# Lightning attention and four-expert MoE on one core: q and k of eight chunks rearranged in DRAM and turned on VectorE, with several smaller edits

## The chip, the cores and the metric

The kernel runs on one core of a Trainium2 chip, in FP32 throughout. A core has a matrix engine (TensorE, PE in the profile; its weight loads are the row PEld), three engines for elementwise work (VectorE or DVE, ScalarE or ACT, GpSimd or POOL), and SyncE (SP), whose queue issues nearly all DMA transfers of this kernel; 16 DMA engines carry them out. TensorE writes into PSUM, eight banks of 128 partitions x 512 FP32 values; DVE and ACT empty them. The metric is the time of one execution on the device in microseconds (us), as a median over runs.

## The reference

Two blocks in a row. The first is a decayed linear attention in blocks of 64 positions, for 4 batches, 8 heads, 768 positions and 64 features:

```
intra = einsum(qb, kb) * Dmask ; intra = einsum(intra, vb)
inter = einsum(qb * lam_pow, kv_state)
out[block] = intra + inter
kv_state = lam**64 * kv_state + einsum(kb * rev_pow, vb)
```

The second is a mixture of four experts with dense gates over the 3072 resulting tokens (512 wide, hidden width 1024):

```
p = domain_probs / (domain_probs.sum(-1) + 1e-9)
for e in range(4):
    out += p[:, e:e+1] * (relu(x @ w1[e]) @ w2[e])
```

## The kernel before

**Attention.** The kernel uses blocks of 128 positions (*chunks*), 6 to a batch, 24 in all. A chunk takes three steps on TensorE. `turn` (line 456) transposes its q and k, each [128 positions, 8 heads x 64], with four 128x128 transposes each into two PSUM banks; ACT copies them out as `qT` and `kT`, DVE makes the decayed `qs` (not for a batch's first chunk), and POOL decays k in place. `scores` (line 479) multiplies `kT` by `qT`, and DVE masks the result into `st`. `values` (line 497) multiplies `st` and the state by v, and the ACT copies bring the result into `xT`, the MoE's input of the present group. A *group* is 8 chunks, so there are three.

**MoE.** A *unit* is one group with one expert, twelve in all, numbered 0 to 11 by `at`. Both of its products (x by w1, and hidden by w2) are two-level Strassen-Winograd schemes with seven products M1 to M7 and sums of blocks as operands. The first product of unit n+1 is interleaved with the second product of unit n. For most units the seven operand sets of x and w1 are made ahead by POOL, stored in DRAM (`x_ops`, `w1_ops`), and read back one set at a time into two buffers (`xs_in`, `ws_in`; `feed`, line 658). Unit 0's first products are made directly from `xT` and from raw w1 blocks (`direct_product`, line 1063), and unit 1's from operands that are made for it in SBUF (`own`, line 1058, with the x sums of `own_x`, line 1004, on DVE). The last group (units 8 to 11) has a deeper scheme for the second product (`nested_product`).

**Order.** Everything is emitted by hand, and each engine runs its instructions in that order. A unit is seven *rounds* of eight *slots*. A slot emits a part of the products; then `rest` takes one item from a list of background work (DVE sums, masks, attention's DVE steps; `soon` puts items at its head), and `pump` takes POOL *chores* and DMA stores that are due. An attention step is placed in slot 5 of each round, and in slot 2 of rounds 1, 3 and 5 (line 1282). Group 1's attention runs in units 0 to 2, and group 2's in units 3 to 5. The SP queue is in order too: a transfer that waits for its buffer holds up those behind it.

**Opening.** The first ten iterations of the loop at line 1124 do group 0's attention with pieces of unit 0's direct products between. Iteration i has `turn` of chunk i, `scores` of chunk i-1 and `values` of chunk i-2, in this order, with `scores` ahead of `turn` in iteration 3 alone. Inputs are loaded in the order q and k of chunks 0 and 1, v0, q and k of 2, v1, q and k of 3, w1 block A11, v2, v3, then chunk 4, A12, chunk 5, A21, chunk 6, A22, chunk 7. In iteration 6 DVE makes the x operands of unit 1's M1 (line 1145). The rest of the direct products follows (lines 1181 to 1191, `SEQ0`).

**Later sums.** `finished` (line 679) queues the sums that follow products M6 and M7. In the last group one of the two operands is first copied into PSUM by ACT (`bring`, line 684), and DVE adds from there.

Of the kernel before, what the change touches and what calls it, by code (L numbers as in the profile page):

```python
# [22 lines left out]
def kernel(  # L23
# [320 lines left out]
    def sum_w1(e, name, a, b, op):  # L344
# [7 lines left out]
        w1_now[e][name] = to  # L352

    lam_bc = consts.tile([P, H], FP32, name="lam_bc")
    nc.scalar.dma_start(out=lam_bc[:], in_=lam.partition_broadcast(P))
    for n, names in ((0, "qk"), (1, "qk"), (0, "v"), (2, "qk"), (1, "v"), (3, "qk")):
        load(n, names)
    raw_w1(0, "A11")
    load(2, "v")
    load(3, "v")  # L360

# [88 lines left out]
    def soon(n, *work):  # L450

        background[0:0] = work
        if n < CPG:
            rest(len(work))

    def turn(n, tags):
        qn, kn = nat.pop((n, "q")), nat[n, "k"]
        qp = bank(tags[0], "qp")
        kp = bank(tags[1], "kp")
        for x, y in ((qp, qn), (kp, kn)):  # L460
            for ac in range(NHP):
                nc.tensor.transpose(  # L462
                    out=x[:, ac * C:(ac + 1) * C], in_=y[:, 2 * ac:2 * ac + 2].rearrange("p r d -> p (r d)"),
                    identity=ident[:],
                )
        qT, kT, qs = small("qT"), small("kT"), None
        nc.scalar.copy(out=qT[:], in_=qp[:])
        nc.scalar.copy(out=kT[:], in_=kp[:])
        if n % NCH:
            qs = small("qs")  # L470
            soon(n, lambda: tt(nc.vector, qs[:], qT[:], q_decay[:].rearrange("p h c -> p (h c)"), ALU.mult))
        turned[n] = qT, kT, qs
        if n % NCH < NCH - 1:

            kd = kn.rearrange("p (ac r) d -> p ac r d", r=2)
            by = k_decay.rearrange("p r ac -> p ac r").unsqueeze(3)
            tt(nc.gpsimd, kd, kd, by.to_broadcast([P, NHP, 2, D]), ALU.mult)

    def scores(n, tags):
        qT, kT, _ = turned[n]  # L480

# [58 lines left out]
    def attention(g):  # L540
# [3 lines left out]
        for n in range(g * CPG, (g + 1) * CPG):  # L544
            steps.append(lambda n=n: turn(n, ("s0", "s1")))
            steps.append(lambda n=n: scores(n, ("s0", "s1")))

            def end(n=n):
                if n == g * CPG:
                    for m in MS:  # L550
                        until(("x", g - 1, m))
                values(n, ("s0", "s1"))
                if n + AHEAD < B * NCH:
                    load(n + AHEAD)
                if n == g * CPG + CPG // 2 - 1:
# [123 lines left out]
    def finished(g, e, m, blocks, new):  # L679

        def later(to, a, b, order, relu=False):
            there = dict(a)

            def bring(at):

                there[at] = bank("s" + "01"[order.index(at) % 2], "up")
                nc.scalar.copy(out=there[at][:], in_=a[at][:])

            def step(at):
                x = there[at]  # L690
                if g == LAST and at != order[-1]:
                    bring(order[order.index(at) + 1])
                o = to[at] if at in to else small("m" + at)
                tt(nc.vector, o[:], x[:], b[at][:], ALU.add)
                if relu:
# [6 lines left out]
            blocks["left"] = 4  # L702
            if g == LAST:
                background.append(lambda: bring(order[0]))
            background.extend(lambda at=at: step(at) for at in order)
# [189 lines left out]
    def to_join(m):  # L895
# [5 lines left out]
        if m == "M3":  # L901
            steps(
                [(bring, "M1", 0, "q01")], [(bring, "M1", 1, "q02"), (add, "M6", "M1", 0)], [(add, "M6", "M1", 1)],
            )
# [99 lines left out]
    def own_x(m):  # L1004
# [14 lines left out]
        else:  # L1019
            if m == "M1":  # L1020
                s = [opool.tile([P, 2, 256], FP32, name="acc") for _ in range(2)]
                parts = ((1, 3), s[0][:]), ((3, 5), s[1][:])
                s = [x[:, i] for x in s for i in range(2)]
            else:
                s = stage.tile([P, 4, 256], FP32, name="ops", tag="st")
                parts = (((1, 5), s[:]),)
                s = [s[:, i] for i in range(4)]
            for n, x, y, op in T_OPS:
                b[n] = s[SLOT[n]]
                tt(nc.vector, b[n], b[x], b[y], op)  # L1030
            pieces = (
                ((0, 1), blk[:, 0:1, 0:256]), *parts, ((5, 7), blk[:, 1].rearrange("p (a f) -> p a f", a=2)),
            )
# [18 lines left out]

    own_ops, own_blocks = {}, {}

# [3 lines left out]
    def own(m):  # L1058
        if m not in own_ops:
            own_weights(m)  # L1060
        fed[0, 1, m] = own_blocks.pop(m, None) or own_x(m), own_ops[m]

    def direct_product(e, m, blocks, tags):

        settle(m, blocks)
        old = {"M1": None, "M5": None, "M6": "M1", "M2": "M1", "M7": "U2", "M3": "U4", "M4": "U3"}[m]
        new = {}

        def quarter(at):
            a, b = w1_now[e][A_OF[m]], x_now[B_OF[m]]  # L1070
            i, j = int(at[0]) - 1, int(at[1]) - 1
# [52 lines left out]
    for i in range(CPG + 2):  # L1124
# [29 lines left out]
        while more:  # L1154
            more.pop(0)()
# [17 lines left out]
    def sum_own(name, a, b, op=ALU.subtract):  # L1173
# [5 lines left out]
        raw["A12"],  # L1179
    ))  # L1180
    for m in SEQ0[2:]:
        if m == SEQ0[-1]:
# [34 lines left out]
    for at, (g, e) in enumerate(units):  # L1217
# [8 lines left out]
        if ahead and ahead[1] == 0:  # L1226
            assert not steps
            steps = attention(ahead[0] + 1) if ahead[0] + 1 < NG else []
        blocks, banks = {}, {}
        for i in range(7):  # L1230
# [30 lines left out]
            for x, part in enumerate(order):  # L1261
# [55 lines left out]
```

## Time and profile before

| What | Value |
|---|---|
| Median of 7 runs | 1196.13 us (1195.42 to 1198.0) |
| The profiled execution | 1197.44 us |
| Its span, first to last instruction | 1195.7 us |
| Busy share of the span: PE, DVE, ACT, POOL | 99%, 66%, 23%, 53% |
| Granted TensorE clock | 1.000 |
| Moved by DMA | 317.94 MB, 266 GB/s |
| Busy share of the 16 DMA engines, main queue (q1) | 77.7% |
| Transposes of q and k (L462), as recorded | 192 of 128x128 |

The share of busy time is over the whole span; which engine decides in a stage is read from the time slices and from the waits. A matrix instruction of the program that multiplies FP32 appears as two matmul records in the trace, and a transpose as one. Matmul records overlap, so the pitch of two starts says more than a record's length. The DMA share by slice lies between 0.4 and 0.99 for most of the run, highest between some 180 and 420 us.

### The profile page before, as it was taken

The numbers are of one execution on the slowest core, as the hardware profiler recorded it, in microseconds if no ns is written. First come the engines' busy times: TensorE is split into PE (matmuls) and PEld (weight loads), VectorE is DVE, ScalarE is ACT, GpSimd is POOL, SyncE is SP. The second block draws the span as 40 slices with busy tenths as digits, with TensorE's granted clock in tenths as the row PEclk, the third lists the DMA queues.
The fourth block names the chain that finished last, engine by engine and source line by source line (L and its number), as shares of the span: only waits on it lengthen the run. The fifth ranks groups of instructions, "written<-read, shape, count | busy, mean of one in ns | idle before, by whom it ended". The sixth has DMA issues, their size and how long they took to land.

```text
span 1195.7 us, 17929 instructions
## 1 busy us (share of the span) xinstructions
PE 1185.4 (99%) x6623; PEld 1030.9 (86%) x6623; DVE 789.6 (66%) x1318; ACT 278.9 (23%) x510; POOL 636.6 (53%) x600
## 2 busy tenths in 40 slices
PE   9999999999999999999999999999999999999998
PEld 8788888888888888888888888888888888888887
DVE  5698786477467746746764874774665676777784
ACT  3322122112212211211211120121243342341332
POOL 1885248349366810034524754416584593783884
PEclk9999999999999999999999999999999999999999
DMA  9794679999999985689977999898986657566542
GB/s 220 222 337 144 224 253 325 354 316 328 366 329 316 328 272 189 218 285 288 282 268 233 320 301 318 277 298 313 321 277 242 260 196 266 214 237 243 211 169 79
DMA packets 228135, 317.94 MB, mean 266 GB/s; under 512 B 91696, under 2 KB 169424, under 8 KB 228048
## 3 DMA queue, kind: packets, MB, share of 16 engines
q1 hardware_dynamic: 218496, 314.11, 77.7%
q10 hardware_dynamic: 9552, 2.69, 1.0%
q8 instruction: 52, 0.85, 0.3%
q14 instruction: 35, 0.29, 0.1%
HBM read 231.40 MB, written 85.34 MB: 265 GB/s over the span
## 4 chain that ended last, share of the span: by engine, by line
PE 92%; DVE 4%; SPq 1%; issue 1%; DMA 1%; POOL 0%; ACT 0%; ACTq 0%; DVEq 0%; POOLq 0%
PE pg L751 39%; PE q L805 32%; PE pq L977 13%; PE sp L485 2%; PE op L513 2%; DVE m L95 1%; DVE hS L95 1%; SPq L123 1%; PE op L508 1%; DVE xt L95 1%; PE op L521 1%; PE pM L1076 1%; PE qp L462 1%; PE kp L462 1%; PE pM L947 1%
## 5 line engine op out<-in xcount | busy, mean ns | idle before, releaser
L751 PE MATMUL pg<-xs_in,ws_in 128*128 128x256 f32 x1960 | 470.0, 380 | 0.5 <-DVE m L95 0.5
L751 PEld LDWEIGHTS pg<-xs_in,ws_in 128*128 128x128 f32 x1960 | 371.0, 190 | 52.3 <-DVE m L95 1.5
L95 DVE TENSOR_TENSOR m<-pg,m 128x512 f32<-128x512 f32 x451 | 308.5, 688 | 113.2 <-PE pg L751 103.9
L805 PE MATMUL q<-w2t,hS 128*128 128x256 f32 x1024 | 243.3, 380 | 0.0
L805 PEld LDWEIGHTS q<-w2t,hS 128*128 128x128 f32 x1024 | 192.9, 190 | 26.8 <-issue 0.3
L821 DVE SCALAR_TENSOR_TENSOR acc<-q,gate,acc 128x256 f32<-128x256 f32 x192 | 92.5, 482 | 178.3 <-PE q L805 177.8
L805 PE MATMUL q<-w2t,m 128*128 128x256 f32 x768 | 182.5, 380 | 0.0
L805 PEld LDWEIGHTS q<-w2t,m 128*128 128x128 f32 x768 | 144.7, 190 | 20.1 <-issue 0.2
L763 ACT ACTIVATE m<-m 128x512 f32<-128x512 f32 x132 | 82.9, 630 | 276.0 <-DVE m L95 268.9
L95 POOL TENSOR_TENSOR m<-m,xT 128x512 f32<-128x512 f32 x64 | 80.6, 1274 | 73.0 <-ACT m L763 55.2
L95 POOL TENSOR_TENSOR kn<-kn,s_decay 128x512 f32<-128x512 f32 x20 | 22.6, 1130 | 166.5 <-PE kp L462 156.6
L95 DVE TENSOR_TENSOR sums<-pq,sums 128x256 f32<-128x256 f32 x154 | 64.8, 422 | 46.2 <-PE pq L977 40.2
L759 ACT COPY m<-pg 128x512 f32<-128x512 f32 x88 | 51.4, 585 | 168.6 <-PE pg L751 163.1
L977 PE MATMUL pq<-acc,w2t 128*128 128x256 f32 x352 | 86.6, 379 | 0.0
L95 POOL TENSOR_TENSOR ops<-w2b 128x256 f32<-128x256 f32 x24 | 18.7, 802 | 109.9 <-DMA w2b<-in_moe_w_dram 101.3
L977 PEld LDWEIGHTS pq<-acc,w2t 128*128 128x128 f32 x352 | 66.8, 190 | 9.3 <-issue 0.3
L95 DVE TENSOR_TENSOR hS<-m,m 128x512 f32<-128x512 f32 x64 | 53.7, 843 | 8.4 <-ACT m L763 8.4
L95 POOL TENSOR_TENSOR acc<-hT,hT 128x512 f32<-128x512 f32 x32 | 40.2, 1272 | 31.2 <-PE pq L977 29.3
L696 ACT ACTIVATE m<-m 128x512 f32<-128x512 f32 x48 | 30.3, 631 | 107.3 <-DVE m L95 107.3
L95 DVE TENSOR_TENSOR m<-m,m 128x512 f32<-128x512 f32 x64 | 54.0, 847 | 0.0
L95 POOL TENSOR_TENSOR w2o<-w2b 128x512 f32<-128x512 f32 x32 | 42.1, 1337 | 15.6 <-DMA w2b<-in_moe_w_dram 10.7
L95 POOL TENSOR_TENSOR acc<-hT,acc 128x512 f32<-128x512 f32 x32 | 40.7, 1271 | 7.4 <-PE pq L977 5.4
(139 smaller groups left out, 1368.6 us busy)
## 6 DMA issues: line engine op xcount, KB each, us to landing
xs_in<-x_ops SPq DMA_DIRECT2D x70, 896.0 KB, 6.1
ws_in<-w_ops SPq DMA_DIRECT2D x70, 896.0 KB, 8.8
w2t<-w_ops SPq DMA_DIRECT2D x66, 256.0 KB, 6.7
w2t<-w_sums SPq DMA_DIRECT2D x64, 256.0 KB, 3.7
w_ops<-ops SPq DMA_DIRECT2D x28, 512.0 KB, 6.3
w2t<-in_moe_w_dram SPq DMA_DIRECT2D x48, 256.0 KB, 3.2
w2b<-in_moe_w_dram SPq DMA_DIRECT2D x32, 256.0 KB, 6.3
w_sums<-w2o SPq DMA_DIRECT2D x16, 512.0 KB, 5.3
```

What stands on the lines that cost most here:

```text
L95: eng.tensor_tensor(out=o, in0=a, in1=b, op=op)
L123: by.dma_start(out=to[:, :, r], in_=of[:, :, r])
L462: nc.tensor.transpose(out=x[:, ac * C:(ac + 1) * C], in_=y[:, 2 * ac:2 * ac + 2].rearrange("p r d -> p (r d)"), identity=ident[:],)
L485: nc.tensor.matmul(out=sp[r][:, ac * C:(ac + 1) * C], lhsT=hc(kT)[half[r], ac], rhs=hc(qT)[half[r], ac], start=True, stop=True,)
L513: nc.tensor.matmul(out=op[r][half[x], a * C:(a + 1) * C], lhsT=vn[:, 4 * r + 2 * a + x], rhs=hc(st[r])[:, 2 * a + x], start=(first and a = ...
L696: nc.scalar.activation(out=o[:], in_=o[:], func=AF.Relu)
L751: nc.tensor.matmul(out=p[:, j * 256:(j + 1) * 256], lhsT=ws[i][:, j * P:(j + 1) * P], rhs=xs[i], start=(fresh and j == 0), stop=True, skip ...
L759: nc.scalar.copy(out=new[at][:], in_=p[:])
L763: nc.scalar.activation(out=new[at][:], in_=new[at][:], func=AF.Relu)
L805: nc.tensor.matmul(out=p[:, s * DH:(s + 1) * DH], lhsT=h[A_OF[m]][:, c * 256 + s * P:c * 256 + (s + 1) * P], rhs=fed2[g, e, m][uu][:, c], ...
L821: nc.vector.scalar_tensor_tensor(out=o, in0=x, scalar=w, in1=o, op0=ALU.mult, op1=ALU.add)
L977: nc.tensor.matmul(out=p[:, 0:256], lhsT=fed3[e, m, x // 2][:, x % 2, c * P:(c + 1) * P], rhs=b[B_OF[i]][:, c * 256:(c + 1) * 256], start= ...
```

## The change

Several edits at once:

- For batches 2 and 3, chunks 2 to 5 of each (chunks 14 to 17 and 20 to 23) no longer use TensorE's transposes. A new DRAM tensor `across` takes their q and k in another order, by 64 transfers from DRAM to DRAM (`bring_across`): 32 for each batch, each 32 rows x 16 x 32 values, 64 KB in pieces of 128 bytes. `load_across` then reads a chunk's q and k back as two transfers of 128 x 4 x 128 values, and k and v also come as before. DVE turns each in 32x32 blocks in place (`nc.vector.transpose`, one instruction of 128x512 for q and one for k), and no PSUM bank or ACT copy is used.
- The 32 transfers of batch 2 are issued one at a time (`trickle`) from the last two direct products on, then in the odd slots of unit 0; those of batch 3 in the odd slots from the start of unit 3. Unit 3, like unit 0, has no attention step in slot 2.
- `scores` takes background items until its q and k are there.
- In the opening, `scores` stands ahead of `turn` in all iterations from 3 on, the pieces of direct products lie between the steps in another way, and w1's blocks are loaded in another order (A12 ahead of v3 and chunk 4, A21 and A22 ahead of chunk 6).
- The x operands of unit 1's M1 are no longer made in iteration 6, but where `own` asks for them, and in a buffer of the `stage` pool.
- `finished` no longer copies an operand into PSUM in the last group.
- Two banks in `to_join` and one condition on `rest` in unit 10 are other ones.

```
+    ACROSS = {2: 2, 3: 2}
+    across = dram.tile([B, 2, P, NHP, NCH * 4, 32], FP32, name="across")
+    def bring_across(b):
+        c = ACROSS[b]
+        for x, of in enumerate((q, k)):
+            for y in range(4):
+                for ac in range(NHP):
+                    src = of[b, 4 * (y // 2) + ac, c * C:, (y % 2) * 32:(y % 2 + 1) * 32]
+                    to = across[b, x, y * 32:(y + 1) * 32, ac, c * 4:]
+                    pieces.append(lambda to=to, src=src: nc.sync.dma_start(
+                        out=to, in_=src.rearrange("(t p) d -> p t d", p=32),
+                    ))
...
+    def load_across(n):
+        b, c = divmod(n, NCH)
+        for x, name in enumerate("qk"):
+            t = small(f"{name}x")
+            nc.sync.dma_start(
+                out=t[:].rearrange("p (h c) -> p h c", c=C),
+                in_=across[b, x, :, :, c * 4:c * 4 + 4].rearrange("p h t d -> p h (t d)"),
+            )
+            nat[n, name + "x"] = t
+
+    def load_more(n):
+        if not comes_across(n):
+            load(n)
+        else:
+            trickle(len(pieces))
+            load_across(n)
+            load(n, "kv")
...
     raw_w1(0, "A11")
     load(2, "v")
+    raw_w1(0, "A12")
     load(3, "v")
...
+    def turn_across(n):
+        qT, kT, kn = nat.pop((n, "qx")), nat.pop((n, "kx")), nat[n, "k"]
+        qs = small("qs") if n % NCH else None
+        def scaled():
+            if n % NCH:
+                tt(nc.vector, qs[:], qT[:], q_decay[:].rearrange("p h c -> p (h c)"), ALU.mult)
+            turned[n] = qT, kT, qs
+        soon(n, *(lambda x=x: nc.vector.transpose(out=x[:], in_=x[:]) for x in (qT, kT)), scaled)
+        if n % NCH < NCH - 1:
+            decayed(kn)
...
     def scores(n, tags):
+        while n not in turned:
+            rest(force=True)
...
-                    load(n + AHEAD)
+                    load_more(n + AHEAD)
...
-            there = dict(a)
-            def bring(at):
-                there[at] = bank("s" + "01"[order.index(at) % 2], "up")
-                nc.scalar.copy(out=there[at][:], in_=a[at][:])
             def step(at):
-                x = there[at]
-                if g == LAST and at != order[-1]:
-                    bring(order[order.index(at) + 1])
...
-                tt(nc.vector, o[:], x[:], b[at][:], ALU.add)
+                tt(nc.vector, o[:], a[at][:], b[at][:], ALU.add)
...
-                [(bring, "M1", 0, "q01")], [(bring, "M1", 1, "q02"), (add, "M6", "M1", 0)], [(add, "M6", "M1", 1)],
+                [(bring, "M1", 0, "q11")], [(bring, "M1", 1, "q12"), (add, "M6", "M1", 0)], [(add, "M6", "M1", 1)],
...
-        fed[0, 1, m] = own_blocks.pop(m, None) or own_x(m), own_ops[m]
+        fed[0, 1, m] = own_x(m), own_ops[m]
...
-        order = [(turn, 0), (scores, 1), (values, 2)]
-        if i == 3:
+        order = [(scores, 1), (turn, 0), (values, 2)]
+        if i < 3:
             order[0:2] = order[1::-1]
         for f, lag in order:
             n = i - lag
-            if more and lag == 0 and i < CPG:
-                more.pop(0)()
             if 0 <= n < CPG:
                 f(n, pairs[n % 3])
...
-            if i == 6 and lag == 2:
-                own_blocks["M1"] = own_x("M1")
...
-            if more and (lag == 2 or i >= CPG):
+            if more:
                 more.pop(0)()
...
-        if i < 3:
-            for name in (("A12",), ("A21",), ("A22",))[i]:
-                raw_w1(0, name)
+        if i == 1:
+            raw_w1(0, "A21")
+            raw_w1(0, "A22")
...
+    bring_across(2)
     for m in SEQ0[2:]:
...
+            if m in SEQ0[-2:]:
+                trickle()
...
+        if at == 3:
+            bring_across(3)
...
-                elif (ahead or x % 2 == 0 and x + i) and not (at == len(units) - 2 and i == 6 and x == 7):
+                elif ahead or x % 2 == 0 and x + i:
                     rest()
...
-                if steps and (at > 0 or i > 1) and (x == 5 or (x == 2 and i in (1, 3, 5) and at > 0)):
+                if steps and (at > 0 or i > 1) and (x == 5 or (x == 2 and i in (1, 3, 5) and at not in (0, 3))):
                     steps.pop(0)()
+                if x % 2:
+                    trickle()
```

More of the change, by code (lines that the diff above doesn't have):

```diff
@@ L352, in sum_w1, with trickle, comes_across @@
         w1_now[e][name] = to
+    ACROSS = {2: 2, 3: 2}
+    across = dram.tile([B, 2, P, NHP, NCH * 4, 32], FP32, name="across")
+    pieces = []
+    def bring_across(b):
[8 more added lines that the diff above has]
+                    ))
+    def trickle(m=1):
+        for _ in range(m):
+            if pieces:
+                pieces.pop(0)()
+    def comes_across(n):
+        b, c = divmod(n, NCH)
+        return b in ACROSS and c >= ACROSS[b]
+    def load_across(n):
+        b, c = divmod(n, NCH)
+        for x, name in enumerate("qk"):
[12 more added lines that the diff above has]
+            load(n, "kv")
     lam_bc = consts.tile([P, H], FP32, name="lam_bc")
@@ L454, in soon, with decayed @@
             rest(len(work))
+    def decayed(kn):
+        kd = kn.rearrange("p (ac r) d -> p ac r d", r=2)
+        by = k_decay.rearrange("p r ac -> p ac r").unsqueeze(3)
+        tt(nc.gpsimd, kd, kd, by.to_broadcast([P, NHP, 2, D]), ALU.mult)
+    def turn_across(n):
[8 more added lines that the diff above has]
+            decayed(kn)
     def turn(n, tags):
+        if comes_across(n):
+            turn_across(n)
+            return
         qn, kn = nat.pop((n, "q")), nat[n, "k"]
@@ L473, in turn @@
         if n % NCH < NCH - 1:
-            kd = kn.rearrange("p (ac r) d -> p ac r d", r=2)
-            by = k_decay.rearrange("p r ac -> p ac r").unsqueeze(3)
-            tt(nc.gpsimd, kd, kd, by.to_broadcast([P, NHP, 2, D]), ALU.mult)
+            decayed(kn)
     def scores(n, tags):
+        while n not in turned:
+            rest(force=True)
         qT, kT, _ = turned[n]
@@ L702, in later @@
             blocks["left"] = 4
-            if g == LAST:
-                background.append(lambda: bring(order[0]))
             background.extend(lambda at=at: step(at) for at in order)
@@ L1019, in own_x @@
         else:
[L1020 to L1027, printed above, removed]
+            s = stage.tile([P, 4, 256], FP32, name="ops", tag="st")
             for n, x, y, op in T_OPS:
-                b[n] = s[SLOT[n]]
+                b[n] = s[:, SLOT[n]]
                 tt(nc.vector, b[n], b[x], b[y], op)
             pieces = (
-                ((0, 1), blk[:, 0:1, 0:256]), *parts, ((5, 7), blk[:, 1].rearrange("p (a f) -> p a f", a=2)),
+                ((0, 1), blk[:, 0:1, 0:256]), ((1, 5), s[:]), ((5, 7), blk[:, 1].rearrange("p (a f) -> p a f", a=2)),
             )
@@ L1051, in keep_own @@
         return lambda: ([nc.sync.dma_start(out=to[:, x:y], in_=of) for (x, y), of in pieces], made.add(what))
-    own_ops, own_blocks = {}, {}
+    own_ops = {}
     def own_weights(m):
@@ L1060, in own @@
             own_weights(m)
-        fed[0, 1, m] = own_blocks.pop(m, None) or own_x(m), own_ops[m]
+        fed[0, 1, m] = own_x(m), own_ops[m]
     def direct_product(e, m, blocks, tags):
+        a, b = w1_now[e][A_OF[m]], x_now[B_OF[m]]
         settle(m, blocks)
@@ L1069, in quarter @@
         def quarter(at):
-            a, b = w1_now[e][A_OF[m]], x_now[B_OF[m]]
             i, j = int(at[0]) - 1, int(at[1]) - 1
@@ L1153 @@
             pump()
-        while more:
-            more.pop(0)()
         if i + 4 < CPG:
             load(i + 4)
-        if i < 3:
-            for name in (("A12",), ("A21",), ("A22",))[i]:
-                raw_w1(0, name)
+        if i == 1:
+            raw_w1(0, "A21")
+            raw_w1(0, "A22")
         if i == 5:
```

## The prediction

> **What bounds the kernel now.** I read the busy times and the chain of waits first, then TensorE's own waits, then the timeline around one removed step, then the time slices where work is added.
>
> ```profile
> PE 1185.4 (99%) x6623; PEld 1030.9 (86%) x6623; DVE 789.6 (66%) x1318; ACT 278.9 (23%) x510; POOL 636.6 (53%) x600
> PE 92%; DVE 4%; SPq 1%; issue 1%; DMA 1%; POOL 0%; ACT 0%; ACTq 0%; DVEq 0%; POOLq 0%
> ...
> PE op L521 <- POOL kn L95: 1.4, 1, 1.4
> PE kp L462 <- DMA kn<-in_k_dram: 0.4, 1, 0.4
> ```
>
> TensorE is without work for 1195.7 - 1185.4 = 10.3 us in the whole span, and 92% of the chain runs on it. A busy PE can hide waits, but the pitch between matmuls is steady outside the opening: so what TensorE need not do comes off the end, unless something new makes it wait. Its two longest waits that the edits touch (the last two lines: waiter, releaser, us, times, longest) lie in the first 60 us.
>
> **What is removed: 64 transposes.** The timeline around one `turn` (chunk 14; start, us, engine):
>
> ```profile
> 269.49 1.89 PE L805 MATMUL q<-w2t,hS 128*128 128x256 f32 x8
> 271.22 0.60 PE L462 MATMUL qp<-ident,qn 128*128 128x128 f32 x4
> 271.66 0.60 PE L462 MATMUL kp<-ident,kn 128*128 128x128 f32 x4
> 272.09 1.89 PE L751 MATMUL pg<-xs_in,ws_in 128*128 128x256 f32 x8
> ```
>
> The step takes 272.09 - 271.22 = 0.87 us, with nothing idle on either side. Eight chunks: -6.96 us, the only term of this size. By its row a transpose costs 0.87 / 8 = 0.109 us. The Trainium skill (VectorE: DVE Perf Modes, The three transpose paths) gives TensorE 390 ns for a 128x128 bf16 transpose, and VectorE 311 ns; by this the 64 would be worth 25 us. The row is this kernel's own pitch and decides.
>
> **What takes their place on DVE.** Two block transposes of 128x512 a chunk, SBUF to SBUF, 16 in all. The trace has none. The nearest rows are other 128x512 instructions within SBUF: 0.68 us for the fast ones, 0.847 the mean of `m<-m`, 1.371 for `xt<-xT`. I take 0.85, as size and memory are those of `m<-m`: 13.6 us of DVE spread over 270 to 630 us, where it is free for over a third of the time (65.2 us busy of 105 from 398 to 503). ACT loses 16 copies of 0.59, off the path. New is that `scores` waits for DVE. By the step rule, six of the eight chunks have five or eight slots between `turn` and `scores`; chunks 22 and 23 have three (slots 2 to 5). There the transposes stand in slots 3 and 4, behind one accumulation of 0.48 us, and slot 5's matmuls take 1.73 us: 0.48 + 0.85 ends in time, and 0.48 + 1.37 is 0.1 late. Queued behind a late `scores` is all of TensorE. If DVE is a whole slot behind, it costs 1.4 us each. Ends 0 and 2.8; I take 0.3, since a DVE that is on time is the rule outside the opening. POOL's decay of k no longer waits for a transpose: nothing, it was never late there.
>
> **Transfers.** Each `bring_across` is 32 x 512 = 16,384 packets of 128 bytes. The smallest mean packets of the page are in the second of these lines (queue: packets, MB, share of 16 engines):
>
> ```profile
> q1 hardware_dynamic: 218496, 314.11, 77.7%
> q10 hardware_dynamic: 9552, 2.69, 1.0%
> ```
>
> 16 x 1195.7 x 1.0% / 9552 = 20 ns for 282 bytes on average, and 68 ns for 1438 bytes on q1; a line through both gives 14 ns at 128. Ends 14 and 68, I take 20 (the nearest row, some 150 bytes too large, but DRAM to DRAM is not in it): 16,384 x 20 / 16 = 20.5 us of all 16 engines for each stretch. The skill's rule against this (DMA: Bandwidth & Descriptors, Specifications) is that below 512 bytes a transfer is done as read-modify-write. Were a packet doubled by it, the estimate would be 41 us and would not fit into the second stretch below. Room there is in the slices (DMA share is the number before the last):
>
> ```profile
> 78.00:165.00 87.00, 85.78 (x448) 74.44 (x447) 72.16 (x116) 16.42 (x29) 39.63 (x38) 1.00 0.61 214
> 398.00:430.00 32.00, 32.00 (x202) 27.72 (x201) 17.02 (x26) 7.78 (x14) 18.94 (x20) 1.00 0.87 309
> 430.00:515.00 85.00, 85.00 (x475) 73.69 (x473) 55.12 (x94) 16.96 (x31) 2.35 (x2) 1.00 0.71 229
> ```
>
> Free are 0.39 x 87 = 33.9 us in the first stretch and 0.13 x 32 + 0.29 x 85 = 28.8 us in the second. What could be late is an operand set:
>
> ```profile
> 387.77 0.34 SPq L666 DMA_DIRECT2D xs_in<-x_ops  x1
> 388.16 0.42 SPq L668 DMA_DIRECT2D ws_in<-w_ops  x1
> ...
> 402.45 1.89 PE L751 MATMUL pg<-xs_in,ws_in 128*128 128x256 f32 x8
> ...
> DMA to landing us min/median/max: 6.1/8.8/11.1
> ```
>
> It is issued 14.3 us ahead of its use and lands after 8.8, at most 11.1, so 3.2 us are left at worst. Four pieces a round are 4 x 512 x 20 / 16 = 2.6 us of the engines, and they are queued behind the set, not ahead of it. On SP 64 issues at 0.5 to 1.0 us (rows of q and v) are 2 to 4 us a round of some 14, in which SP mostly waits; behind them stand stores and the next w2 tiles, which are two products ahead. The reading back is 512 packets for q instead of 1024, and k comes twice; the first is needed 100 us after its pieces, the second set is complete a round before. For all of it 0 to 4 us; I take 0.6.
>
> **The opening.** Three moves. (1) A12 goes ahead of chunk 4, whose k TensorE already awaited until 21.05. At 221 GB/s (the slice from 0 to 60) 512 KB are 2.4 us; by the issue times of its two transfers 1.05. `scores`, now ahead of `turn`, covers 1.1 us. Net 0 to 1.4: +0.8. (2) A21 and A22 come a chunk's load earlier (issues at 26.85 to 29.7), so POOL's w1 sums, which began at 34.98 when A22 had landed, begin some 3 us sooner, and the 1.4 us wait for POOL's `kn` behind them goes: -1.4 to 0, I take -1.2. (3) The four x sums for unit 1's M1 move from 42.7-47.9 us, where DVE had time, to the end of the direct products, where it has none:
>
> ```profile
> 60.00:97.00 37.00, 36.57 (x170) 32.19 (x171) 36.83 (x48) 9.72 (x17) 33.20 (x25) 1.00 0.81 270
> ...
> 91.51 0.68 DVE L95 TENSOR_TENSOR m<-pM,m 128x512 f32<-128x512 f32 x1
> 94.18 1.03 PE L751 MATMUL pg<-acc,ops 128*128 128x256 f32 x4
> ```
>
> In the changed program they stand on DVE just ahead of the sum at 91.51, which empties the bank that the matmuls at 94.18 fill. They cost 2 x 0.416 + 2 x 0.629 = 2.1 us by the rows of the same sums in unit 0, and 5.2 beside POOL's 128x512 sums (the rows `acc<-xT`, 1.35 and 1.27). The bank is free at 94.3 or 97.4: 0.1 to 3.2 us late, next to be late is the second product's bank at 95.04. I take 0.9, near the low end, since POOL runs 128x256 sums there, beside which DVE's took 0.67. The other order of pieces costs nothing: each `scores` still has a piece or `values` ahead of it, which hides the two ACT copies (1.2 us, and 1.2 each if that cover were gone).
>
> **The last group.** 32 sums go from 0.680 (`m<-up,m`) to 0.847 (`m<-m,m`): 5.3 us of DVE over four units, in which TensorE waits for 1.3 us altogether. 0 to 2, I take 0.4. ACT's 32 copies go, off the path. The banks in `to_join` and the condition on `rest`: nothing, other work of DVE hides them; 0.5 each if not. Unit 3's missing slots put group 2's last attention step two rounds later, and POOL's x sums with it, about 680 instead of 652; they are read from 790 on.
>
> **The sum.** -6.96 + 0.3 + 0.6 + 0.8 - 1.2 + 0.9 + 0.4 = -5.2 us. Against the profiled execution: 1197.44 - 5.2 = 1192.3. That execution lies 1.3 above the median of its runs (1196.13), so the forecast for the median is **1191.0 us**.
>
> **Rivals.**
> *The opening and DVE give it back* (no change). For: DVE is busy 36.83 of 37 us where the sums go; all dear ends together are 2.8 + 1.4 + 3.2 + 2 without the 1.2 gained, 9.4 against 6.96. Against: they lie at different places, and each has a reason for its cheap end. At about half of them, 4.7 us beside 0.6 for transfers, the median is 1196.1 - 7.0 + 5.3 = 1194.4; 1195 with one dear end more.
> *The pieces fill the DMA engines* (slower). Place: units 3 and 4. From 28.8 x 16 / 16,384 = 28 ns a packet the second stretch has no room. At 45 ns it needs 46 us, 17 too many; less the 3.2 of slack, TensorE waits some 14 us for operand sets: 1191.0 + 14 = 1205. At 68 ns it is nearer 1228. For: no DRAM to DRAM packet is in the trace, and the share is 0.87 where it starts. Against: small packets are the cheap ones there.
> *It doesn't do what it says*: TensorE waits out the 0.87 us that each `turn` took, as DVE comes late each time; 1196 to 1198. For: DVE is in order behind its other sums. Against: five or more slots for six of eight. It is counted with the first rival.
>
> **How the numbers follow.** The forecast has 0.68, no change 0.17, the full DMA engines 0.15. About 0.2% (2.4 us) is what a measurement of this kernel can tell from no change: faster means below 1193.7, slower above 1198.5. The range runs from 1188.0 (only the gains, 1196.1 - 7.0 - 1.2) to 1196.5, which takes in most of no change.
>
> **What would show it.** Right: L462 falls from 192 to 128 records; a product follows a product where `turn` stood; TensorE's waits for DVE at `scores` are below 1 us in sum; the wait of L521 for POOL is gone. Wrong: waits of TensorE for `ws_in` or `xs_in` in units 3 and 4 with landings above 14 us, a DMA share near 1 from 400 to 510, block transposes above 1.4 us, or more than 3 us of idle TensorE around 94 us.

## The result, and the profile after

| | Before | After |
|---|---|---|
| Median, measured beside each other | 1196.81 us (1194.91 to 1199.04, 35 runs) | 1194.01 us (1192.43 to 1194.91, 14 runs) |
| The profiled execution, and its span | 1197.44, 1195.7 | 1194.18, 1192.4 |
| Records of q's and k's transposes on TensorE | 192 | 128 |
| Granted TensorE clock | 1.000 | 1.000 |

The ratio is 0.9975, with a 95% interval of 0.9968 to 0.9982: the changed kernel is faster by 0.25%, 2.8 us by the two medians. The forecast was a gain of 5.2 us.

The busy times and the chain of waits of the changed kernel:

```profile
PE 1179.9 (99%) x6559; PEld 1023.5 (86%) x6559; DVE 807.5 (68%) x1334; ACT 253.3 (21%) x462; POOL 635.9 (53%) x600
PE 88%; DVE 6%; DMA 2%; POOL 1%; SPq 1%; issue 1%; ACT 0%; ACTq 0%; DVEq 0%; POOLq 0%
```

TensorE is busy for 5.5 us less than before (1185.4), but the span fell by 3.3 only. The other 2.2 are new idle time: 12.5 us instead of 10.3. The chain says on which engine to look: DVE holds 6% of it instead of 4%.

To see where, I matched the same matmuls of two traces by their source line and order, and took how much later or earlier each starts than in the kernel before, counted from the first matmul. Negative is earlier. The columns are places, in the time of the kernel before; all kernels but the first are experiments told below:

```
offset (us) at      58     88    120    330    700   1035   1185
after            -1.22  -2.28   1.04   1.04  -4.95  -5.09  -3.16
across_alone     -1.03  -1.94   1.88   1.88  -4.07  -4.25  -4.24
no_across        -1.07  -1.78  -0.90  -0.83  -0.79  -0.93   0.99
own_early        -1.30  -2.35  -0.83  -0.83  -6.82  -6.96  -5.03
pieces_later     -2.16  -2.79  -1.78  -1.78  -7.36  -7.51  -5.58
acc_tiles        -1.62  -2.41   0.62   0.62  -5.30  -5.44  -3.52
psum_last        -1.22  -2.18   0.42   0.42  -5.85  -6.03  -5.19
double_pieces    -1.78  -2.67   0.78   5.41   8.25   8.12  10.04
all_back         -1.42  -1.76  -2.33  -1.98  -7.38  -7.56  -7.56
both_back        -1.77  -2.83  -1.61  -1.61  -7.62  -7.40  -7.40
ten_chunks       -1.75  -2.34  -4.06  -5.48 -11.92 -12.10 -12.09
```

The first line is the whole result. The stretch with the eight chunks (330 to 700) gains 6.0 us. Between 88 and 120 us 3.3 us are lost, and in the last group 1.9. The 2.28 us at 88 can't be read off one pair of traces: `across_alone`, which keeps the opening's old order, has 1.94 there too, in an execution that was 1.8 us shorter than its median. The profiled execution of the kernel before, against which all lines stand, was a long one (1197.44, its median 1196.1 to 1196.8), and single traces differ by such amounts. I read differences of 1 us and less from several kernels together or not at all.

The medians say that a part of these 2.28 us does belong to the change. Behind 88 us the first line adds up to 3.32 - 5.99 - 0.14 + 1.93 = -0.9 us, and the medians differ by 2.8: an estimate of 1.9 us is left for the opening. Worked out in the same way, seven experiments that keep the opening's new order leave a gain of 1.5 to 2.1 us, `no_across` leaves 0.5, `ten_chunks`, whose runs scatter widely, a loss of 1.0, and `across_alone`, with the old order, a loss of 0.3. So the new order probably gains up to 2 us; no run has it by itself.

**The eight chunks.** The timeline of DVE at chunk 14, where its q and k are turned (start, us, engine, line, operation):

```profile
339.86 0.70 DVE L517 STREAM_TRANSPOSE qx<-qx 128x512 f32<-128x512 f32 x1
340.49 0.65 DVE L95 TENSOR_TENSOR m<-pg,m 128x512 f32<-128x512 f32 x1
341.06 0.69 DVE L517 STREAM_TRANSPOSE kx<-kx 128x512 f32<-128x512 f32 x1
```

A block transpose takes 0.70 us, about what a 128x512 sum takes, and the MoE's sums go on between the two. TensorE's waits between 360 and 700 us (waiter, releaser, us, times, longest), of which the kernel before had none:

```profile
PE pg L806 <- DVE m L95: 1.2, 3, 0.5
```

So `scores` never waited; three times a bank of the MoE's product was emptied late by DVE, which has the transposes to do besides. The pieces made no operand set late. The windows that answer to those of before (stretch, us, PE, PEld, DVE, ACT, POOL, clock, DMA share, GB/s):

```profile
78.00:165.00 87.00, 83.44 (x433) 71.23 (x432) 71.29 (x114) 16.21 (x28) 41.32 (x39) 1.00 0.75 236
430.00:515.00 85.00, 85.00 (x481) 73.64 (x481) 55.77 (x95) 15.01 (x27) 2.95 (x4) 1.00 0.84 253
```

The DMA share rose from 0.71 to 0.84 in the last one and TensorE is busy for all of it. From 380 to 640 us `ws_in` lands 7.4 to 10.4 us after its issue, 9.2 in the middle. The loss is in the first line: PE 83.44 of 87, before 85.78.

**The loss around 95 us.** TensorE's waits for DVE at the MoE's product `pg`, from 60 to 120 us, before and now (before there were another 0.8 us at a direct product, ahead of 88 us):

```profile
PE pg L751 <- DVE m L95: 1.1, 1, 1.1
PE pg L806 <- DVE m L95: 3.1, 3, 1.2
```

The timeline there: one line of POOL in the kernel before, then the changed kernel, POOL first, then DVE and PE:

```profile
76.62 6.18 POOL L95 TENSOR_TENSOR w2o<-w2b,w2o 128x512 f32<-128x512 f32 x4
...
66.80 3.14 POOL L95 TENSOR_TENSOR w2o<-w2b 128x512 f32<-128x512 f32 x2 [0.93 <-DMA w2b<-in_moe_w_dram]
80.90 3.20 POOL L95 TENSOR_TENSOR w2o<-w2b 128x512 f32<-128x512 f32 x2 [10.96 <-DMA w_sums<-w2o]
84.17 6.36 POOL L95 TENSOR_TENSOR w2o<-w2b,w2o 128x512 f32<-128x512 f32 x4
...
83.49 2.83 DVE L95 TENSOR_TENSOR hS<-m,m 128x512 f32<-128x512 f32 x2
87.92 2.90 DVE L95 TENSOR_TENSOR ops<-xT 128x256 f32<-128x256 f32 x2
90.85 1.70 DVE L95 TENSOR_TENSOR ops<-xT,ops 128x256 f32<-128x256 f32 x2
92.47 0.68 DVE L95 TENSOR_TENSOR m<-pM,m 128x512 f32<-128x512 f32 x1
...
93.30 1.10 PE L806 MATMUL pg<-ops 128*128 128x256 f32 x4 [1.24 <-DVE m L95]
```

The moved x sums of unit 1's M1 are the two `ops` lines of DVE: 4.6 us, where the forecast had 2.1 (its dear end 5.2). The bracket with `w_sums` says why they meet POOL's four sums `w2o<-w2b,w2o` in this trace: POOL stood idle for 10.96 us and begins them at 84.17 instead of 76.62. Beside POOL's 128x512 sums a DVE sum of two SBUF operands takes two to three and a half times as long: `ops<-xT` 1.45 us instead of 0.42, `hS<-m,m` 1.41 instead of 0.67. `m<-pM,m`, with an operand in PSUM, keeps its 0.68. The Trainium skill (SBUF — State Buffer, SBUF: two separate sides) has a rule for this: a DVE instruction with two SBUF inputs and a POOL instruction that reads SBUF exclude each other for a whole instruction. These rows agree with it.

### The profile page after: what moved, and what is told of

The parts are those of the page before. It is cut to its first block, busy times and chain, and to the rows that moved or that the text cites. A ratio compares the mean times of both kernels' runs of the same rounds, so it can differ in the third digit from the quotient of the medians.

```text
span 1192.4 us, 17827 instructions
## 1 busy us (share of the span) xinstructions
PE 1179.9 (99%) x6559; PEld 1023.5 (86%) x6559; DVE 807.5 (68%) x1334; ACT 253.3 (21%) x462; POOL 635.9 (53%) x600
## 4 chain that ended last, share of the span: by engine, by line
PE 88%; DVE 6%; DMA 2%; POOL 1%; SPq 1%; issue 1%; ACT 0%; ACTq 0%; DVEq 0%; POOLq 0%
PE pg L806 37%; PE q L860 31%; PE pq L1032 12%; DVE m L95 3%; PE op L580 2%; PE sp L552 2%; DVE hS L95 2%; PE pM L1124 1%; PE op L575 1%; SPq L123 1%; PE op L588 1%; DMA w_sums<-w2o 1%; PE pM L1002 1%; POOL m L95 1%; PE kp L530 0%
## 5 line engine op out<-in xcount | busy, mean ns | idle before, releaser
L95 DVE TENSOR_TENSOR sums<-pq,sums 128x256 f32<-128x256 f32 x154 | 64.4, 422 | 45.7 <-PE pq L1032 39.9
L95 DVE TENSOR_TENSOR m<-m,m 128x512 f32<-128x512 f32 x96 | 83.6, 875 | 0.0
```

What stands on the lines that cost most here:

```text
L95: eng.tensor_tensor(out=o, in0=a, in1=b, op=op)
```

## The experiments

Each was timed beside the kernel before on the same chip, in 5 to 12 runs; the ratio is to that.

| Label | Median, us | Ratio, 95% interval |
|---|---|---|
| own_early | 1192.40 | 0.9962, 0.9948 to 0.9975 |
| pieces_later | 1192.20 | 0.9955, 0.9943 to 0.9967 |
| psum_last | 1192.14 | 0.9958, 0.9945 to 0.9970 |
| across_alone | 1195.12 | 0.9979, 0.9970 to 0.9988 |
| acc_tiles | 1193.61 | 0.9974, 0.9963 to 0.9984 |
| no_across | 1198.87 | 1.0019, 1.0011 to 1.0028 |
| double_pieces | 1207.34 | 1.0091, 1.0077 to 1.0104 |
| all_back | 1188.87 | 0.9935, 0.9922 to 0.9948 |
| both_back | 1191.09 | 0.9953, 0.9939 to 0.9968 |
| both_back_act | 1195.65 | 0.9990, 0.9975 to 1.0004 |
| ten_chunks | 1188.38 | 0.9936, 0.9914 to 0.9959 |
| twelve_chunks | 1213.29 | 1.0137, 1.0112 to 1.0162 |

The theory was that the eight chunks gain what they should, and that two places give half of it back: DVE at the end of the direct products, because of the moved x sums, and the last group, because of the dearer sums. The first rival was that the pieces, not the sums, cost in the opening.

**own_early: the moved sums back to iteration 6**

```
+    if m == "M1":
+        s = [opool.tile([P, 2, 256], FP32, name="acc") for _ in range(2)]
...
+            if i == 6 and lag == 2:
+                own_blocks["M1"] = own_x("M1")
```

> The changed kernel with one part undone: the four x sums for unit 1's M1 are made in iteration 6 again, in the two accumulator tiles. In the two profiles the same matmuls run 2.3 us earlier than before at 92 us and 1.0 us later at 102 us, so 3.3 us are lost there. Theory 'the moved sums': they cost all of it, since DVE has no time there; the time falls by about 3.3 us, to 1190.7 (before: 1196.8, changed: 1194.0), and TensorE's waits for DVE between 60 and 120 us fall from 3.1 us to under 1. Rival 'late POOL': the pieces ahead of the w2b loads hold POOL up, and its large sums slow every DVE sum there; then under half of it comes back, 1192.5 to 1194.

1192.4. In the trace 1.9 of the 3.3 us came back (offset at 120 us: -0.83). DVE's `m` is then still late, by up to 2.2 us at 104 us. The sums account for about half of that loss.

**pieces_later: no pieces in the last two direct products**

```
-            if m in SEQ0[-2:]:
-                trickle()
```

> The changed kernel without pieces in the last two direct products: the first stretch starts with unit 0, later by 10 pieces. Theory 'the moved sums': the four sums still stand where DVE has no time, so less than 1 us comes back, 1193 to 1194. Rival 'late POOL': POOL's 128x512 w2 sums, which ran from 84 to 90.5 us here and from 76.6 to 82.8 before, are on time again, the four sums take 2.1 us instead of 4.6, and some 2.5 us come back: 1191.5.

1192.2, and 2.8 us back at 120 us. Most of the loss is gone, but not as the rival had it: the moved sums are where they were, and they still take 4.6 us, in `no_across` too. So early pieces are not what makes them dear: POOL runs 128x512 sums beside the last two of them here as well (`w1o<-w1o,w1b`, 2.86 us from 88.43). POOL's wait for the store `w_sums` is 7.6 us instead of 11.0. What changed is the place of POOL's last two w2 blocks in SP's queue. These are its issues in the changed kernel, then here, and then the last two of the moved sums here:

```profile
73.30 1.07 SPq L240 DMA_DIRECT2D w2b<-in_moe_w_dram  x2
67.59 0.92 SPq L240 DMA_DIRECT2D w2b<-in_moe_w_dram  x2
...
88.79 2.78 DVE L95 TENSOR_TENSOR ops<-xT,ops 128x256 f32<-128x256 f32 x2
```

The kernels with early pieces and the new opening (own_early, both_back) issue the two blocks at 72.9 to 73.5 us, those without (all_back, no_across) at 68.5 to 69.6. They land 4.0 to 5.4 us after their issue in all of them. So the blocks come late because they are issued late, and not because the DMA engines are fuller.

**acc_tiles: the moved sums stay, in two other tiles**

```
-            s = stage.tile([P, 4, 256], FP32, name="ops", tag="st")
+            if m == "M1":
+                s = [opool.tile([P, 2, 256], FP32, name="acc") for _ in range(2)]
...
```

The sums took one of the stage buffers in which POOL stores its w2 sums. This run frees it and moves nothing.

> The changed kernel with the four moved x sums left where they are, but written into two accumulator tiles instead of a buffer of the stage pool. In the changed kernel's trace POOL's w2 sums wait 11.0 us for a store of w_sums that holds the next stage buffer, and then run beside the four sums. Theory 'the buffer': that wait shrinks to the few us for w2b that the kernel with early sums shows, the four sums take 2 to 3 us instead of 4.6, and 1.5 to 2.5 us come back: 1191.5 to 1192.5. Rival 'no time on DVE': the place decides and not the buffer, less than 0.7 us comes back, 1193.3 or above.

1193.61: no change that can be told from the changed kernel. POOL's wait of 11.0 us is gone; it waits 4.0 us for `w2b` instead. The timeline of DVE and PE:

```profile
89.60 1.81 DVE L95 TENSOR_TENSOR acc<-xT 128x256 f32<-128x256 f32 x2
91.45 1.69 DVE L95 TENSOR_TENSOR acc<-xT,acc 128x256 f32<-128x256 f32 x2
...
93.89 1.10 PE L806 MATMUL pg<-acc,ops 128*128 128x256 f32 x4 [1.96 <-DVE m L95]
```

The sums still take 3.5 us, and TensorE waits 1.96 in one piece. So the place of the sums costs, with or without the buffer.

**across_alone and no_across: the two halves of the change**

`across_alone` is the kernel before with the rearranged q and k (`bring_across`, `load_across`, `turn_across`, the pieces at the changed kernel's places, unit 3 without steps in slot 2) and none of the other edits. `no_across` is the changed kernel with

```
-    ACROSS = {2: 2, 3: 2}
+    ACROSS = {}
...
-    bring_across(2)
...
-        if at == 3:
-            bring_across(3)
```

> The kernel before with only the rearranged q and k of the eight chunks, all other edits left out. Theory 'the terms add up': 8 x 0.87 = 6.96 us less of TensorE and 0.8 us of small waits, -6.2 us: 1190.6, from a time before of 1196.8. Rival 'pieces cost in the opening stage': the pieces delay POOL's w2 sums here too, and 2 us or more are lost between 60 and 110 us: 1192.5 or above.

> The changed kernel with no chunk rearranged (no pieces, TensorE turns all 24 chunks), with all its other edits. Theory 'the gain is TensorE's 64 transposes': from the kernel that has its pieces later (1192.2) the 6.2 us that the eight chunks gave come back on top: 1198.4, 1 to 2 us slower than the kernel before. Rival 'the other edits carry part of the gain': 1195 to 1196.8, level with or under the kernel before.

`no_across` is 1198.87, slower than before: the other edits lose 2.3 us. Its ratio against that of the changed kernel puts the eight chunks at 0.44%, 5.3 us; its offset does not move between 330 and 700 us, where the changed kernel's falls by 6.0.

`across_alone` missed. It keeps the early sums and should have had the whole gain, 1190.6; it measured 1195.12 (one of its eleven runs took 4388 us, which the median does not feel). Between 88 and 120 us it lost 3.8 us. Its waits from 60 to 120 us:

```profile
PE pg L817 <- DVE m L95: 3.5, 2, 3.0
...
POOL w2o L95 <- DMA w2b<-in_moe_w_dram: 3.9, 3, 1.7
```

POOL waited 1.5 us for `w2b` before. The pieces stand between these loads on SP's queue, POOL's w2 sums come later, and at 101 us four sums `xt<-xt` of DVE took 3.06 us, 1.79 in the kernel before. Moved sums alone cost too. From 88 to 120 us, by the offsets:

| Early pieces | Moved sums | Lost from 88 to 120 us |
|---|---|---|
| no | no | none; 0.6 and 1.7 gained (all_back, ten_chunks) |
| no | yes | 0.9, 1.0 (no_across, pieces_later) |
| yes | no | 1.2, 1.5, 3.8 (both_back, own_early, across_alone) |
| yes | yes | 2.6 to 3.5 (the changed kernel, psum_last, acc_tiles, double_pieces) |

Both causes are shown. Why across_alone, the one with the opening's old order, loses so much more than the two others in its row is open; without it the two causes about add up.

**psum_last: ACT's copies into PSUM again, in the last group**

```
+            there = dict(a)
+            def bring(at):
+                there[at] = bank("s" + "01"[order.index(at) % 2], "up")
+                nc.scalar.copy(out=there[at][:], in_=a[at][:])
...
-                tt(nc.vector, o[:], a[at][:], b[at][:], ALU.add)
+                tt(nc.vector, o[:], x[:], b[at][:], ALU.add)
...
```

> The changed kernel with the ACT copies into PSUM in the last group back. Matmuls lose 1.9 us against the kernel before from 1040 us to the end. Theory 'dearer sums': the 32 sums within SBUF (0.875 us as mean against 0.680) cost 1.4 to 1.9 of it: 1192.1 to 1192.6. Rival 'the other tail edits' (two banks, one condition on rest): nothing comes back, 1194.0.

1192.14. In the last group 0.8 us are lost instead of 1.9. Of the sums from 1040 us on, eight `m<-m,m` at 0.942 us are `m<-up,m` at 0.681 again. What stays lost is at two matmuls, which stand in the changed kernel's timeline as

```profile
1141.86 2.83 PE L1032 MATMUL pq<-acc,w2t 128*128 128x256 f32 x12 [0.51 <-POOL m L95]
...
1154.92 2.83 PE L1032 MATMUL pg<-acc,w2s 128*128 128x256 f32 x12 [0.58 <-DVE sums L95]
```

These go with the two banks in `to_join` and the condition on `rest`: `all_back`, which takes those edits back too, loses nothing after 1035 us. Which of the two costs what was not tried.

**double_pieces: twice as many pieces of half the size**

```
+                    for z in (slice(0, 16), slice(16, 32)):
+                        pieces.append(lambda to=to[:, :, z], src=src[:, z]: nc.sync.dma_start(
...
-                    trickle()
+                    trickle(2)
```

The bytes stay, packets and transfers double: 65,536 packets of 64 bytes in place of 32,768 of 128.

> The changed kernel with every piece cut into two of 64-byte packets: 128 transfers and 65,536 packets, two issued where one was (in the opening still one by one). Theory 'transfers are hidden': packets of 128 bytes took 13 ns in the trace, so halves of some 11 add 32,768 x 11 x 2 / 16 - 32,768 x 13 / 16 = 18 us of all 16 engines over some 200 us, and TensorE waits for no operand set: within 0.7 us of the changed kernel, 1193.3 to 1194.7. Rival 'the engines or SP are nearly full in units 3 and 4': waits for xs_in or ws_in appear, 1196 or above.

1207.34, the theory missed by 13 us. The trace has this wait, of which the kernel before has none:

```profile
PE pg L807 <- DMA ws_in<-w_ops: 10.3, 5, 5.0
```

It looks like full DMA engines and is not. From 430 to 515 us their share is 0.81, against 0.84 in the changed kernel, since a packet of 64 bytes takes 11 ns and one of 128 bytes 13 (medians). SP's queue ahead of the longest wait, which ends at 468.27:

```profile
443.42 6.79 SPq L368 DMA_DIRECT2D across<-in_q_dram  x4
450.26 2.37 SPq L123 DMA_DIRECT2D qn<-in_q_dram  x2
...
454.32 2.65 SPq L368 DMA_DIRECT2D across<-in_q_dram  x4
...
459.46 0.42 SPq L736 DMA_DIRECT2D ws_in<-w_ops  x1
```

SP has no pause: it issues for 16 us, and 9.4 of them are eight pieces. The operand set, the nineteenth of its kind, goes out at 459.46; in the changed kernel at 446.96. That is 12.5 us later; 4 of them were lost by 330 us, and the set ahead of it was 10.0 late already. It lands in the usual time (8.7 us in the middle of this stretch, 9.5 at most). So the set is late because it is issued late. What is not shown is why some issues are so long: the middle one of all 128 takes 0.63 us, but one of the first four above takes 3.79. The changed kernel has such issues as well, up to 3.48.

**all_back: what the runs above asked for**

The early sums of own_early, the copies of psum_last, pieces_later, and the old banks and condition of the end. What remains of the change is the opening's order and the eight chunks.

> The changed kernel with the early x sums, the ACT copies into PSUM with the two tail edits, and no pieces in the last two direct products: the opening's new order and the eight chunks are what is left of the change. Theory 'independent losses': -2.3 us from the opening to 92 us, -6.2 from the eight chunks, nothing lost from 92 to 110 and at the end: 1196.8 - 8.5 = 1188.3. Rival 'the losses share a cause': the gains overlap, and it stays at 1190 or above.

1188.87, a ratio of 0.9935: it beats both kernels, and the sum of the single returns holds. Its busy times, and TensorE's longest group of waits in the whole run:

```profile
PE 1178.5 (99%) x6559; PEld 1022.6 (86%) x6559; DVE 803.5 (68%) x1334; ACT 271.1 (23%) x494; POOL 635.4 (53%) x600
```

```profile
PE pg L818 <- DVE m L95: 2.2, 3, 0.9
```

TensorE idles for 1188.1 - 1178.5 = 9.6 us, less than before the change.

**both_back and both_back_act: pieces in the direct products, on SP's queue or on ACT's**

`both_back` is all_back without the edit of pieces_later. `both_back_act` differs from it in one word:

```
-                    pieces.append(lambda to=to, src=src: nc.sync.dma_start(
+                    pieces.append(lambda to=to, src=src: nc.scalar.dma_start(
```

> The version all_back with one edit taken back: the 32 transfers of batch 2 start in the last two direct products again, as in the changed kernel, on SP's queue. Theory (the transfers hold up SP's queue there, and with it the w2 blocks and POOL's sums, whatever DVE does at that place): slower than all_back's 1188.9 by 1 to 2 us, 1189.9 to 1190.9. Rival (they cost only where the moved x sums stand there too): within 0.5 of all_back, 1188.4 to 1189.4.

> As both_back, and all 64 transfers are issued on ACT's queue instead of SP's; same places in the program, same bytes, same packets. Theory (it is SP's queue that they hold up): what both_back loses comes back, 1188.4 to 1189.4, less whatever ACT's own copies lose by 64 issues of some 0.6 us; POOL's waits for w2 blocks between 60 and 120 us return to those of all_back. Rival (the 16 DMA engines, or the DRAM, are what they hold up): the same as both_back, within 0.5 us.

`both_back` measured 1191.09, 2.2 us above all_back where the theory had 1 to 2; but its six runs lie between 1188.92 and 1194.31, the intervals overlap, and the two traces end within 0.2 us of each other. In the stretch itself, from 88 to 120 us, both_back loses 1.2 us and all_back gains 0.6. It speaks for the theory and does not settle it.

`both_back_act` missed both: 1195.65. The pieces now stand in ACT's order, the first at 84.7 us instead of 64.4, and three engines wait on that. SP's next load of q takes 13.8 us to issue, because it waits for a piece to land; POOL waits 11.4 us for a store that is queued behind it; and an ACT copy that empties a bank stands for 10.4. The DMA share from 60 to 97 us is 0.69 in this kernel and 0.90 in `both_back`, which is faster. So it is the order of issues again and not full engines, but as a test of SP's queue by itself the run was a poor one: the two queues are tied by the program. In the trace the load waits for a completion semaphore that it shares with a piece on ACT's queue.

**ten_chunks and twelve_chunks: more of the same**

Both are all_back with more chunks:

```
ten_chunks:
-    ACROSS = {2: 2, 3: 2}
+    ACROSS = {2: 0, 3: 2}
twelve_chunks:
+    ACROSS = {2: 0, 3: 0}
-        if at == 3:
+        if at == 2:
             bring_across(3)
```

> The version all_back with chunks 12 and 13 rearranged too: ten chunks in place of eight, the same number of transfers, batch 2's of 96 KB in place of 64, so 24,576 packets in the first stretch. Theory (a chunk turned on DVE is worth 0.87 us of TensorE, as eight were worth 6.2 of 6.96): 1188.9 - 1.5 to 1.75 = 1187.1 to 1187.4. Rival (these chunks are needed so early that their transfers are flushed at once, and SP's queue stands): 1188.9 or above, with a wait of TensorE for xs_in, ws_in or for kx or qx in units 0 to 2.

> As ten_chunks with chunks 18 and 19 too, batch 3's transfers starting in unit 2 instead of 3: twelve chunks. Theory: 1188.9 - 12/8 of the part above eight, 4 x 0.77 to 0.87 = 3.1 to 3.5: 1185.4 to 1185.8. Rival (between 240 and 400 us the DMA engines are busy above 0.9, and the transfers in unit 2 make operand sets late there): 1187.5 to 1190, with TensorE's waits for ws_in or xs_in between 240 and 400 us.

`ten_chunks` measured 1188.38, but its seven runs lie between 1185.37 and 1197.12, and its interval (0.9914 to 0.9959) holds all_back's. In the trace, its shortest execution, the two chunks gain 1.75 us between 250 and 330, as they should, and no operand set is late. By the clock it is unclear whether it beats all_back.

`twelve_chunks` is slower than everything, far beyond the rival's 1190. The timeline, SP first, then PE:

```profile
330.93 8.23 SPq L367 DMA_DIRECT2D across<-in_q_dram  x10
339.19 11.42 SPq L367 DMA_DIRECT2D across<-in_k_dram  x16
...
358.39 0.45 SPq L735 DMA_DIRECT2D ws_in<-w_ops  x1
...
367.11 3.75 PE L818 MATMUL pg<-xs_in,ws_in 128*128 128x256 f32 x8 [20.98 <-DMA ws_in<-w_ops]
```

Chunk 18 is wanted before its pieces have trickled out, so `load_across` issues the 26 that are left in a row: 19.7 us in which SP does nothing else; most of them take 0.65 each. The operand set goes out 33.7 us later than the same one in ten_chunks (324.72), where TensorE was 10.6 us ahead already; it lands within 12 us, and TensorE stands for 21. The DMA share from 330 to 352 us is 0.89: the rival named the right tile and the wrong resource. Starting the pieces of batch 3 earlier still was not tried.

## Why the forecast was right, and where its steps were not

The direction was right for its main reason, and 1194.01 is within the range. The size was not: 2.8 us in place of 5.2. Two terms for what is given back were too small, and one cost was expected at another place. It was a near thing, too. By the forecast's own bound faster meant below 1193.7, counted from 1196.1; beside the kernel before as measured with it, 1196.81, the gain is just above the 2.4 us that the forecast called clear of no change. The interval, which ends at 0.9982, leaves no doubt of the direction.

- **64 transposes, -6.96.** Right. 6.0 us in four kernels between 330 and 700 us (after, across_alone, own_early, both_back) and 5.4 to 6.4 in five others, after waits; double_pieces, both_back_act and twelve_chunks lose time there to other waits. The lines that the forecast gave as chunk 14's are chunk 12's, which keeps its transposes. Chunk 14's step starts at 336.50 us and takes 0.87 us as well, so the sum stands.
- **DVE, +0.3.** The instruction was priced too high (0.85; 0.70), the wait too low and at the wrong step: not `scores` but the emptying of the product's banks, 1.2 us in three waits. That is the 0.9 between 6.96 and 6.0.
- **Transfers, +0.6.** Units 3 and 4 as forecast: no set late. The packet was priced at 20 ns and took 13, so the rival "the pieces fill the DMA engines" had no ground, and a rule that the forecast weighed against the change, that a transfer below 512 bytes is done as read-modify-write (the Trainium skill, DMA: Bandwidth & Descriptors, Specifications), shows in no time here: medians of 11, 13, 18 and 27 ns for 64, 128, 256 and 512 bytes. What failed is the sentence on SP, that behind the pieces stand only stores and w2 tiles that are two products ahead. In the first stretch w2 blocks for POOL stand there, and POOL's sums behind them come later and meet DVE's: 1.2 to 3.8 us in the traces with pieces and early sums (own_early, both_back, across_alone). And issues, not packets, are what runs out when there are more (double_pieces, twelve_chunks): 0.63 us in the middle, 0.8 as the mean.
- **Opening, (1) and (2), -0.4.** Probably more than that. The wait of L521 for POOL is gone, as forecast; in across_alone, with the old order, it is 0.7 instead of 1.4. In the traces the changed kernel is only 0.3 better than across_alone at 88 us, but the medians leave an estimate of 1.9 us. If so, it was luck that some 1.5 us more here covered a part of what the other terms had too small.
- **Opening, (3), +0.9.** The term that was mis-sized. Mechanism and place were named; the low end was chosen because POOL runs 128x256 sums there. In the changed kernel POOL is late and 128x512 sums lie there: the sums take 4.6 us, near the dear end. Without the pieces they take as much and cost the 0.9 of the forecast (no_across), so that figure agrees by luck; with the pieces the stretch loses 3.3. The sign that the forecast named for being wrong, more than 3 us of idle TensorE around 94 us, came in part: its waits at `pg` from 60 to 120 us are 3.5 us, and were 1.1 before.
- **Last group, +0.4.** Mis-sized: 1.9. The dearer sums took 0.90 us (mean of the 32 from 780 us on) against 0.847 forecast and cost 1.1; the edits at the end, priced at nothing "because other work of DVE hides them", cost 0.8.

Summed up by the offsets: -2.28 + 3.32 - 5.99 - 0.14 + 1.93 = -3.16 us, which is the difference of the two profiled executions (3.26) to 0.1. By the medians the first term is the estimate of -1.9, and the sum -2.8. The rival "the opening and DVE give it back" had 1194.4, nearer than the forecast, and its mechanism is what ate half the gain; of its places two came true (x sums, last group), and `scores` did not.

## What to carry to other kernels

Price a transfer twice: once by its bytes on the DMA engines, and once as an issue on its queue, with a list of who is queued behind it at that place. A moved piece of work has to be priced beside the neighbours it will have after the change, not those in the old trace; here sums priced at 2.1 us took 4.6 at their new place. When a mixed change gains less than it should, take the parts back one by one: four of its edits cost 0.40% together, 4.8 us, and without them the gain is more than twice as large.

## What the runs showed of the hardware beyond that

- The issue of a rearranging transfer of 64 to 96 KB takes 0.56 to 0.65 us on SP in most cases, that of `ws_in` with its 896 KB 0.42. What these transfers cost their queue does not go by their bytes.
- Half the bytes in a packet save little: 13 to 11 ns from 128 to 64 bytes.
- In this program, transfers issued on ACT's queue held up SP's: a load of q on SP waited 13 us for a piece that ACT had still to issue, by a completion semaphore that both use.
